# One round of a spectral loop, with two pieces of vector work moved to a later step

## The chip, the cores and the metric

The kernel runs on one core of a Trainium2 chip. The metric is device time in microseconds (us) of one execution. A core has engines with instruction queues of their own, each worked in order: PE (matrix products), DVE and ACT (vector and scalar work), POOL (here copies and the issue of many DMAs) and SP (the issue of other DMAs). They wait for each other through semaphores. The timeline calls a queue's DMA issues SPq, ACTq or POOLq.

## The reference

The reference is a forward pass and its gradients, for one input `x` of 2048 rows by 1024 columns:

```python
g = _sigmoid((x * gate_w).sum(-1, keepdims=True))
a = _A_ref(x, A_w_r, A_w_i)              # irfft2(rfft2(x) * (w_r + 1j * w_i))
b = _B_ref(x, B_w1, B_b1, B_w2, B_b2)    # relu(x @ w1 + b1) ** 2 @ w2 + b2, 3584 hidden
return g * a + (1 - g) * b
```

The outputs are this result and, for a given `grad_out`, the gradients of x, both spectral weights, both MLP weights and biases, and the gate's weights. Here `x` is `A_x`; the MLP's input `B_x` is held constant.

## The kernel before, in words

One main stream of matrix products keeps PE filled: first the MLP's hidden layer and its gradient (`mlp_in`), then the gradients of the weights (`mlp_grads`), then the outputs (`Outputs`). The spectral part is a side stream, a Python generator that is dealt into the main one. `spread` (L1778) runs the main generator and, after each of its yields, advances the side stream by as many steps as are due. While the loop of this change runs beside `mlp_in`, `first_rate` (L1909) makes 1.5 steps due per main yield, so deals of one and of two steps alternate. A main piece is a unit of four yields (`Unit`, L920): seven short chains of four matmuls (tiles ph and pZ, L927) and four chains of eight for the gradient (tile pd, L826). DVE and ACT empty their PSUM banks: DVE writes rT (L946) and dhT (L830), ACT the copies cu and u. A chain that needs a bank waits for that work.

The spectral part has three stages: `first_stage` transforms rows, `fft_mid` (L333) does the column transform, multiplies by the filter and goes back, and `fft_out` transforms the rows back. `fft_mid` is a loop of `NM` = 16 rounds (L532), each for a pair of row groups m and 32 - m, in eight steps with a yield behind each. Each round handles two halves of the columns, h = 1 (which the change's words call the first) and then h = 0. In a round before the change:

- Step 1: `spectra` (L431) multiplies the sums pm and z of both halves into px on PE, after the main stream's last matmul; `grads_of_w` (L493) of the last round's half 0 on DVE (g, gs); `transform` (L441) copies px of half 1 to x on ACT; the loads of next round's z, half 1, are issued on ACT's queue (L404).
- Step 2: the same transform and loads for half 0.
- Step 3: `products` (L448) of half 1, two DVE multiplications of x by the filter w into tt; `by_groups` (L407) reorders the filter of half 0 on POOL (L410, L417).
- Step 4: `rows_of` (L468), the back products of the previous round's y on PE into pv, both halves; `copy_of` (L477) copies half 1 of pv to vc on ACT; results of the weights' gradient are scaled and stored; `filters` (L388) issues loads on POOL's queue.
- Step 5: `joined` (L456), which adds the products to y, half 1; `back` (L483), two DVE operations from pv and vc to pc, and the store of pc to `y_scr` on POOL's queue (L491).
- Step 6: `grads_of_w` of half 1; `mirrored` (L420), sum and difference of next round's z of half 1 on DVE (L426), the difference in place; vc of half 0.
- Step 7: `mirrored` for half 0; `back` of half 0.
- Step 8: `products` and `joined` of half 0; the filter of next round's half 1 on POOL; more scaling.

px and pv share two PSUM buffers (tag `ps2`), so the px of a half also follows the pc that empties the pv of that half. x, w, z, y, pm and pc have two buffers each, tt one, which `grads_of_w` shares (its tile g).

The program text isn't the order of an engine's queue. The build lays out the queues from the data dependences, with the text's order as priority and its own estimate of times, so an operation that it takes to be ready can go ahead of an earlier one. `after`, `behind` and `in_turn` (L250 to L264) add order edges without a wait. The mirrored sums of half 1 have such an edge behind `summed`, the last of `grads_of_w`; px has one behind the main stream's last matmul.

Of the kernel before, what the change touches and what calls it, by code (L numbers as in the profile page):

```python
# [141 lines left out]
def kernel(  # L142
# [98 lines left out]
    def columns_of(scr, c, h):  # L241
        return scr[:].rearrange("t c r x h l -> c h (r x) t l")[c, h]
# [7 lines left out]
    def after(ins, earlier, wait=mybir.DependencyClass.Sync):  # L250

        if earlier is not None:
            info = mybir.DependencyInfo(wait, mybir.DependencyReason.DATA)
            tc.add_manual_dep(ins.ins, earlier.ins.name, info, reason="paced")
# [5 lines left out]
    def behind(ins, eng):  # L260
        after(ins, ahead[eng], mybir.DependencyClass.NoSync)
# [71 lines left out]
    def fft_mid(filler):  # L333
# [63 lines left out]
        def inputs(m, h, copied=None):  # L397
            z = fb.tile([P, 2, 2, HW], FDT, name="z", tag="z", bufs=2)
            for n, c in enumerate((m, R1 // 2 + m)):
                from_ = columns_of(z_scr, c, h)  # L400
                if copied is None:
                    ld(out=z[:, n], in_=from_)
                else:
                    after(nc.scalar.dma_start(out=z[:, n], in_=from_), copied, mybir.DependencyClass.NoSync)  # L404
            return z

        def by_groups(h, wn):  # L407

            w = fb.tile([P, 3, WL], BF16, name="w", tag="w", bufs=2)
            first_ = G.tensor_copy(  # L410
                out=w[:, 0:2, 0:HW].rearrange("p c (g i) -> p c g i", g=4),
                in_=wn[:, :, h * HW : (h + 1) * HW].rearrange("p c (i g) -> p c g i", g=4),
            )
            after(first_, later["mats"], mybir.DependencyClass.NoSync)
            if h:
                after(G.tensor_copy(out=w[:, 0:2, HW], in_=wn[:, :, H]), first_, mybir.DependencyClass.NoSync)
            G.tensor_scalar(out=w[:, 2, 0 : HW + h], in0=w[:, 1, 0 : HW + h], scalar1=-1.0, scalar2=None, op0=ALU.mult)  # L417
            return w

        def mirrored(m, z, summed=None):  # L420

            if m == 0:
                return z[:, 0], z[:, 1]
            pm = fb.tile([P, 2, HW], FDT, name="pm", tag="pm", bufs=2)
            for out, op in ((pm[:], ALU.add), (z[:, 1], ALU.subtract)):
                mixed = V(out=out, in0=z[:, 0], in1=z[:, 1], op=op)  # L426
                behind(mixed, "DVE")
                after(mixed, summed, mybir.DependencyClass.NoSync)
            return pm[:], z[:, 1]

        def spectra(m, pm):  # L431
            px = fps.tile([P, 2, 2, HW], FP32, name="px", tag="ps2", bufs=2)
            for c in range(2):
                for n in range(2):
                    one = mm(px[lanes[n], c], lhsT=mats[m][:, 0, n, lanes[c]], rhs=pm[n], start=True, stop=True)
                    behind(one, "PE")
                    if c + n == 0:
                        in_turn(one, "PE")
            return px

        def transform(m, h, px, ex):  # L441
            x = fb.tile([P, 3, 2, WL], FDT, name="x", tag="x", bufs=2)
            nc.scalar.copy(out=x[:, 1:3, :, 0:HW], in_=px[:])
            copied = nc.scalar.mul(out=x[:, 0, :, 0:HW], in_=px[:, 1], mul=-1.0)
            after(nc.scalar.copy(out=x[:, :, :, h * HW], in_=ex[:, m, :, :, h]), copied, mybir.DependencyClass.NoSync)  # L445
            return x, copied

        def products(h, x, w):  # L448
            tt = fb.tile([P, 2, 2, 2, WL], FDT, name="tt", tag="tt")
            W = HW + h  # L450
            for k, (a, b) in enumerate(((1, slice(0, 1)), (0, slice(1, 3)))):
                by = w[:, b, 0:W].rearrange("p (o t) l -> p o t l", o=1).to_broadcast([P, 2, 2, W])
                V(out=tt[:, k, :, :, 0:W], in0=x[:, a : a + 2, :, 0:W], in1=by, op=ALU.mult)  # L453
            return tt
# [13 lines left out]
        def rows_of(m, y):  # L468
            pv = fps.tile([P, 2, 2, HW], FP32, name="pv", tag="ps2", bufs=2)
            for c in range(2):  # L470
                for n in (1, 0):
                    one = mm(pv[:, n], lhsT=mats[m][lanes[n], 1, c, :], rhs=y[lanes[n], c], start=c == 0, stop=c == 1)
                    if c == 0 and n:
                        in_turn(one, "PE")
            return pv

        def copy_of(m, pv):  # L477
            if m == 0:
                return None, None
            vc = fb.tile([P, 2, HW], FP32, name="vc", tag="vc")  # L480
            return vc, nc.scalar.copy(out=vc[:], in_=pv[:, 1])

        def back(m, h, pv, vc):  # L483
            pc = fb.tile([P, 2, 2, HW], FDT, name="pc", tag="pc", bufs=2)
            if m == 0:
                nc.scalar.copy(out=pc[:], in_=pv[:])
            else:
                V(out=pc[:, 0], in0=pv[:, 0], in1=vc[0][:], op=ALU.add)  # L488
                V(out=pc[:, 1], in0=pv[:, 0], in1=vc[0][:], op=ALU.subtract)
            for n, c in enumerate((m, R1 // 2 + m)):  # L490
                st(out=columns_of(y_scr, c, h), in_=pc[:, n])  # L491

        def grads_of_w(h, x):  # L493
            W = HW + h
            XA, XB = x[:, 0:2, 0, 0:W], x[:, 1:3, 1, 0:W].unsqueeze(1).to_broadcast([P, 2, 2, W])
            part, *inner = XA.ap
            XA = bass.AP(tensor=XA.tensor, offset=XA.offset, ap=[part, inner[0], *inner])
            gs = fb.tile([P, 2, WL], FDT, name="gs", tag="gs", bufs=2)
            t_ = fb.tile([P, 2, 2, 2, WL], FDT, name="g1", tag="tt")[:, 0]
            V(out=t_[:, :, :, 0:W], in0=XB, in1=XA, op=ALU.mult)  # L500
            summed = V(out=gs[:, ::-1, 0:W], in0=t_[:, :, 0, 0:W], in1=t_[:, :, 1, 0:W], op=ALU.add)
            return gs, summed
# [16 lines left out]
        z = {1: inputs(0, 1)}  # L519
# [7 lines left out]
        w = {1: by_groups(1, wn[0])}  # L527
        z[0] = inputs(0, 0)
        pm = {h: mirrored(0, z[h]) for h in (1, 0)}
        x, y, gs, was = {}, {}, {}, None  # L530
        yield
        for m in range(NM):  # L532
            more = m + 1 < NM
            px = {h: spectra(m, pm[h]) for h in (1, 0)}
            if m:
                gs[0], _ = grads_of_w(0, x[0])
            x[1], copied = transform(m, 1, px[1], ex)
            if more:
                z = {1: inputs(m + 1, 1, copied)}
            yield  # L540
            x[0], copied = transform(m, 0, px[0], ex)
            if more:
                z[0] = inputs(m + 1, 0, copied)
            yield
            tt = products(1, x[1], w[1])
            w[0] = by_groups(0, wn[m])
            yield
            if m:
                pv = {h: rows_of(m - 1, y[h]) for h in (1, 0)}
                vc = copy_of(m - 1, pv[1])  # L550
                grads_out(m - 1, 0, gs[0], gw, copied)
            if more:
                wn[m + 1] = filters(m + 1)
            yield
            eh = fb.tile([P, 2, 2], FDT, name="eh", tag="eh")
            y[1] = joined(1, tt, eh)
            if m:
                back(m - 1, 1, pv[1], vc)
            yield
            gs[1], summed = grads_of_w(1, x[1])  # L560
            if more:
                pm = {1: mirrored(m + 1, z[1], summed)}
            if m:
                vc = copy_of(m - 1, pv[0])
            yield
            if more:
                pm[0] = mirrored(m + 1, z[0])
            if m:
                back(m - 1, 0, pv[0], vc)
            yield  # L570
            tt = products(0, x[0], w[0])
            y[0] = joined(0, tt, eh)
            if more:
                w[1] = by_groups(1, wn[m + 1])
            gw = fb.tile([P, 2, LW], BF16, name="gw", tag="gw", bufs=2)
            grads_out(m, 1, gs[1], gw, vc[1] if m else None)
            yield
        gs[0], _ = grads_of_w(0, x[0])
        yield
        for h in (1, 0):  # L580
            pv = rows_of(NM - 1, y[h])
            vc = copy_of(NM - 1, pv)
# [1387 lines left out]
```

## Time and profile before

| What | us |
|---|---|
| median of 3 runs | 1192.29 |
| lowest and highest of them | 1190.86, 1193.34 |
| the profiled execution, its own time | 1196.52 |
| its span, first to last instruction | 1194.7 |
| PE busy in the span | 1173.5 |
| DVE busy in the span | 897.9 |
| first and last start of px in the trace | 225.1, 561.9 |

The trace is one execution. A timeline line gives start, duration, engine, source line, operation, the tile written and those read, the partitions and elements, and, in brackets, how long the engine was idle just before and what ended that. A line of waits gives the engine and line that waited, for whom, the total, how often and the longest. A line of a helper stands for all its callers; L426, for instance, is both the sum (`pm`) and the difference (`z`) in `mirrored`. Some matmul records are missing from the trace, a few per cent, so a chain of eight can show as seven, and PE's idle time is a little overstated.

### The profile page before, as it was taken

What the parts mean: (1) busy time and instruction counts of PE and PEld (TensorE: products, weight loads), DVE (VectorE), ACT (ScalarE), POOL (GpSimd) and SP (SyncE); (2) the same over time, 40 slices, a digit from 0 to 9 for tenths busy, and PEclk for the clock granted to TensorE, in tenths of its full rate; (3) what the DMA queues carried; (4) which work ended last, traced back from release to release, by engine and by line L of the source; (5) the groups of instructions that cost most, each with busy time, mean ns of one, the idle gap of its engine ahead of it and who ended that gap; (6) DMA issues with size and microseconds to landing.
All of it is one profiled execution on the core that took longest, in us unless ns stands there. A gap on an engine that the chain in (4) does not pass through costs nothing.

```text
span 1194.7 us, 19383 instructions
## 1 busy us (share of the span) xinstructions
PE 1173.5 (98%) x7181; PEld 640.3 (54%) x7275; DVE 897.9 (75%) x1598; ACT 531.0 (44%) x961; POOL 387.9 (32%) x618
## 2 busy tenths in 40 slices
PE   8999999999999999999999999999999999999998
PEld 5555555444433444444446999998544444444444
DVE  6898887788988797877537666676786777976757
ACT  5678788577676773445224665664210010000000
POOL 0233443556666683764231333221001100000000
PEclk9999999999999999999999999999999999999999
DMA  9997675687979879889997999995889998564530
GB/s 264 287 306 215 187 203 167 196 219 180 206 186 198 253 250 184 200 187 219 208 198 165 238 226 251 243 216 153 258 188 267 238 277 272 176 194 149 180 124 36
DMA packets 329464, 249.84 MB, mean 209 GB/s; under 512 B 187912, under 2 KB 287658, under 8 KB 328858
## 3 DMA queue, kind: packets, MB, share of 16 engines
q1 hardware_dynamic: 268352, 112.12, 45.1%
q0 software_dynamic: 35136, 111.72, 29.6%
q10 hardware_dynamic: 25882, 24.76, 7.1%
q8 instruction: 57, 0.93, 0.3%
q14 instruction: 37, 0.30, 0.1%
HBM read 114.82 MB, written 89.67 MB: 171 GB/s over the span
## 4 chain that ended last, share of the span: by engine, by line
PE 69%; DVE 16%; DMA 5%; ACT 4%; issue 4%; POOL 1%; SPq 1%; ACTq 0%; another core or an unknown queue 0%; DVEq 0%; POOLq 0%
PE pX L1256 15%; PE xX L1557 14%; PE pV L1256 11%; PE pd L826 8%; PE xV L1557 7%; PE ph L927 4%; PE xZ L1557 3%; PE ph L819 2%; DVE rT L946 2%; DVE dhT L830 1%; DVE tt L453 1%; PE pui L325 1%; PE pki L634 1%; DMA z<-z_scr 1%; PE pu L325 1%
## 5 line engine op out<-in xcount | busy, mean ns | idle before, releaser
L826 PE MATMUL pd<-dbT,w2T 128*128 128x512 bf16 x860 | 206.5, 379 | 7.8 <-DVE rT L946 2.5
L826 PEld LDWEIGHTS <-w2T 128*128 128x128 bf16 x896 | 86.3, 98 | 110.4 <-issue 10.3
L1557 PEld LDWEIGHTS <-dS 128*128 128x128 f16 x686 | 66.4, 98 | 79.4 <-issue 3.8
L830 DVE SCALAR_TENSOR_TENSOR dhT<-pd,rT 128x512 bf16<-128x512 f32 x112 | 76.6, 684 | 31.6 <-PE pd L826 29.2
L1608 POOL DMA_DIRECT2D out_dram<-ot x32 | 17.4, 544 | 248.6 <-DVE ot L1664 128.0
L1674 ACT ACTIVATE w2br<-w2br,dsc 128x512 f32<-128x512 bf16 x8 | 5.8, 723 | 178.6 <-DVE ot L1664 117.4
L1557 PE MATMUL xX<-oT,dS 128*128 128x512 f16 x336 | 76.4, 379 | 0.6 <-DVE eR L1586 0.5
L1272 ACT COPY u<-pX 128x512 f32<-128x512 f32 x56 | 32.8, 586 | 90.8 <-PE pX L1256 85.2
L1557 PEld LDWEIGHTS <-odd 128*128 128x128 bf16 (+1 forms) x462 | 44.8, 98 | 51.5 <-issue 0.9
L1557 PEld LDWEIGHTS <-even 128*128 128x128 bf16 (+1 forms) x448 | 43.6, 98 | 52.6 <-issue 0.7
L1256 PEld LDWEIGHTS <-T 128*128 128x128 f16 x672 | 64.6, 98 | 7.5 <-issue 0.2
L947 ACT ACTIVATE rT<-rT 128x512 bf16<-128x512 bf16 x69 | 43.4, 629 | 50.2 <-DVE rT L946 49.8
L794 ACT ACTIVATE h2T<-rT 128x1024 bf16<-128x1024 bf16 x56 | 59.6, 1064 | 0.2
L1276 DVE TENSOR_TENSOR whi<-pV,u 128x512 bf16<-128x512 f32 x28 | 19.3, 689 | 47.1 <-ACT u L1272 47.0
L1256 PEld LDWEIGHTS <-S 128*128 128x128 f16 x336 | 32.5, 98 | 40.8 <-DVE S L1188 1.9
L491 POOL DMA_DIRECT2D y_scr<-pc x64 | 47.2, 738 | 18.1 <-DVE pc L488 11.1
L453 DVE TENSOR_TENSOR tt<-x,w 128x1028 f16<-128x1028 f16 (+1 forms) x64 | 42.6, 699 | 10.5 <-ACT x L445 4.5
L1256 PEld LDWEIGHTS <-resL 128*128 128x128 bf16 x448 | 43.1, 98 | 4.9
L1256 PEld LDWEIGHTS <-resR 128*128 128x128 f16 (+1 forms) x448 | 42.9, 98 | 4.9 <-issue 0.2
L1276 DVE TENSOR_TENSOR wlo<-pV,u 128x512 bf16<-128x512 f32 x28 | 19.2, 687 | 32.0 <-PE pV L1256 31.9
L858 POOL DMA_DIRECT2D h2T_scr<-h2T x28 | 20.9, 746 | 66.9 <-ACT f L285 29.2
L239 POOL DMA_DIRECT2D r<-y_scr x48 | 28.0, 588 | 41.9 <-ACT re L613 33.1
(382 smaller groups left out, 2798.0 us busy)
## 6 DMA issues: line engine op xcount, KB each, us to landing
h2T_scr<-h2T POOLq DMA_DIRECT2D x28, 512.0 KB, 4.3
dhT_scr<-dhT POOLq DMA_DIRECT2D x28, 512.0 KB, 6.0
y_scr<-pc POOLq DMA_DIRECT2D x64, 128.0 KB, 4.3
ax_scr<-yo POOLq DMA_DIRECT2D x16, 512.0 KB, 5.1
out_dram<-ot POOLq DMA_DIRECT2D x31, 256.0 KB, 3.7
z<-z_scr ACTq DMA_DIRECT2D x60, 128.0 KB, 4.2
out_dram<-whi POOLq DMA_DIRECT2D x28, 256.0 KB, 4.9
out_dram<-wlo POOLq DMA_DIRECT2D x28, 256.0 KB, 5.6
```

The costliest lines, as they stand in the source:

```text
L239: st(out=a, in_=b) if stored else st(out=b, in_=a)
L453: V(out=tt[:, k, :, :, 0:W], in0=x[:, a : a + 2, :, 0:W], in1=by, op=ALU.mult)
L491: st(out=columns_of(y_scr, c, h), in_=pc[:, n])
L794: after(nc.scalar.activation(h2T, rT, ACT.Square), behind_, mybir.DependencyClass.NoSync)
L826: turn["PE"] = mm(pd[:], lhsT=w_[:, ec, fc % FGC * P : (fc % FGC + 1) * P], rhs=dbT[:, ec, ss], start=(ec == 0), stop=(ec == DC - 1),)
L830: return STT(out=dhT, in0=pd[:], scalar=2.0, in1=rT, op0=ALU.mult, op1=ALU.mult, accum_out=gb1part[:, fc, sb : sb + 1],)
L927: turn["PE"] = mm(acc[:], lhsT=lhs[:, t, :], rhs=rhs[:, t, :], start=start and t == 0, stop=t == KH - 1, skip_group_check=True,)
L947: nc.scalar.activation(rT, rT, ACT.Relu)
L1256: self.mm = mm(out, lhsT=lhs[:, t, m * P : (m + 1) * P], rhs=rhs[:, t, :], start=start and t + a == 0, stop=t == KH - 1, skip_group_check= ...
L1272: turn["ACT"] = nc.scalar.copy(out=t_[:], in_=self.X[:])
L1276: turn["DVE"] = self.added = V(out=self.half(row, j), in0=self.sums(acc), in1=self.sums(t_), op=ALU.add)
L1557: ins = mm(acc, lhsT=lhs[:, fc, :], rhs=rhs[:, fc, :], start=start and fc == 0, stop=fc == KH - 1 and bias is None, skip_group_check=True,)
```

## The change

In every round, `products` of half 1 goes from step 3 to step 4, where it stands ahead of the back products; step 3 keeps only the reordering of the filter. The copy vc of half 0 stays in step 6; `back` of half 0 stays in step 7 and becomes its first work. The mirrored sums of half 1 go from step 6 to step 7, behind `back`, and those of half 0 from step 7 to step 8, ahead of the products and the join there. A round keeps eight steps.

```diff
@@ -542,9 +542,9 @@
             if more:
                 z[0] = inputs(m + 1, 0, copied)
             yield
+            w[0] = by_groups(0, wn[m])
+            yield
             tt = products(1, x[1], w[1])
-            w[0] = by_groups(0, wn[m])
-            yield
             if m:
                 pv = {h: rows_of(m - 1, y[h]) for h in (1, 0)}
                 vc = copy_of(m - 1, pv[1])
@@ -558,16 +558,16 @@
                 back(m - 1, 1, pv[1], vc)
             yield
             gs[1], summed = grads_of_w(1, x[1])
+            if m:
+                vc = copy_of(m - 1, pv[0])
+            yield
+            if m:
+                back(m - 1, 0, pv[0], vc)
             if more:
                 pm = {1: mirrored(m + 1, z[1], summed)}
-            if m:
-                vc = copy_of(m - 1, pv[0])
             yield
             if more:
                 pm[0] = mirrored(m + 1, z[0])
-            if m:
-                back(m - 1, 0, pv[0], vc)
-            yield
             tt = products(0, x[0], w[0])
             y[0] = joined(0, tt, eh)
             if more:
```

More of the change, by code (lines that the diff above doesn't have):

```diff
@@ L544, in fft_mid @@
             yield
-            tt = products(1, x[1], w[1])
             w[0] = by_groups(0, wn[m])
             yield
+            tt = products(1, x[1], w[1])
             if m:
@@ L560, in fft_mid @@
             gs[1], summed = grads_of_w(1, x[1])
-            if more:
-                pm = {1: mirrored(m + 1, z[1], summed)}
             if m:
@@ L565, in fft_mid @@
             yield
+            if m:
+                back(m - 1, 0, pv[0], vc)
+            if more:
+                pm = {1: mirrored(m + 1, z[1], summed)}
+            yield
             if more:
                 pm[0] = mirrored(m + 1, z[0])
-            if m:
-                back(m - 1, 0, pv[0], vc)
-            yield
             tt = products(0, x[0], w[0])
```

## The prediction, made before the changed kernel ran

> **What bounds the kernel now.** I read the page first, then the busy time by stretches, then the waits of PE and of DVE in the stretch that the change touches, then the timeline around the longest of them. The page's first part, and the table by stretches (span part, then busy us of PE, PEld, DVE, ACT, POOL, then clock and DMA):
>
> ```profile
> PE 1173.5 (98%) x7181; PEld 640.3 (54%) x7275; DVE 897.9 (75%) x1598; ACT 531.0 (44%) x961; POOL 387.9 (32%) x618
> ...
> 225.00:450.00 225.00, 217.83 (x1049) 93.05 (x1070) 195.48 (x413) 162.48 (x288) 146.56 (x224) 1.00 0.82 208
> 450.00:575.00 125.00, 123.75 (x592) 53.60 (x600) 96.95 (x150) 51.59 (x101) 67.29 (x94) 1.00 0.92 198
> ```
>
> PE is idle for 1194.7 - 1173.5 = 21.2 us of the whole span; that is all that any reordering can win. The loop `for m in range(NM)` (L532) runs from the first px at 225.1 us to past the last at 561.9. Its first twelve rounds lie beside the units of the MLP (225 to 450), where PE is idle 7.2 us and DVE is busy 195.48 of 225, 87%. The later rounds lie beside the weight gradients, where PE is idle 1.25 us in 125. So only 225 to 450 can pay much. PE's waits there (who waited for whom: us in total, times, longest):
>
> ```profile
> PE pd L826 <- DVE rT L946: 2.5, 3, 1.5
> PE pd L826 <- DVE dhT L830: 2.5, 5, 0.7
> PE ph L927 <- ACT u L934: 0.6, 2, 0.3
> PE ph L927 <- DVE rT L946: 0.4, 1, 0.4
> ```
>
> They sum to 6.0 us. None is a wait for the spectral work itself: PE stands because DVE is late with the main stream's rT and dhT, which free PE's banks. Why is DVE late? Its own waits in the same stretch:
>
> ```profile
> DVE pm L426 <- DMA z<-z_scr: 5.0, 4, 2.7
> DVE tt L453 <- issue: 4.5, 3, 2.0
> DVE tt L453 <- ACT x L445: 4.2, 5, 1.3
> DVE tt L453 <- POOL w L410: 0.9, 1, 0.9
> ```
>
> 14.6 us in which the in-order DVE stands at a mirrored sum or at a product of the first half, with rT and dhT queued behind. The longest, first on DVE, then on PE:
>
> ```profile
> 377.42 0.42 DVE L426 TENSOR_TENSOR pm<-z 128x512 f16<-128x512 f16 x1
> 380.55 0.42 DVE L426 TENSOR_TENSOR pm<-z 128x512 f16<-128x512 f16 x1 [2.71 <-DMA z<-z_scr]
> 380.89 0.74 DVE L946 SCALAR_TENSOR_TENSOR rT<-pZ,b1col,cu 128x512 bf16<-128x512 f32 x1
> ```
> ```profile
> 378.28 1.89 PE L927 MATMUL ph<-dbn,Sw 128*128 128x512 f16 x8
> 381.69 1.89 PE L826 MATMUL pd<-dbT,w2T 128*128 128x512 bf16 x8 [1.51 <-DVE rT L946]
> 383.91 1.02 PE L927 MATMUL ph<-dbn,Sw 128*128 128x512 f16 x4 [0.34 <-ACT u L934]
> ```
>
> The sum waits 2.71 us for z (its last transfer was issued at 369.81 and took over 10 us; the stretch's median is 4.7), rT stands behind it, and PE loses 1.51 and then 0.34 us.
>
> **The change part by part.** No instruction, byte or buffer is added or removed. The eight steps of a round keep their number, so the dealing of steps to the main stream is as before. Moved are per round: four mirrored sums (two pairs; one follows the next in 0.34 us) and two products (0.69 each). No DMA changes its step: the loads of z (ACT's queue, steps 1 and 2), the filters and the stores of gw (POOL) stay; the stores of y on POOL come with their pc, which now stands ahead of the sums. SP issues nothing of it.
>
> *Mirrored sums behind pc.* I trace each PE stall back along DVE to the last idle in front of it. Behind waits for z: 0.40 at 259.24 (after 0.39 idle), 0.60 at 318.88 (after 1.45), 1.51 + 0.34 at 381.69 and 383.91 (after 2.71). Sum 2.85 us. After the change the two pc, ready by then (vc was copied before the sums in the last two), run first: 2 x 0.60 = 1.2 us of useful work inside the wait. At 252.92 pc is ACT's (round 0's rows), and a dhT of the main stream fills the 0.39. The 0.43 at 358.90 closes; of the 1.45 there remain 0.25 and of the 2.71 some 1.5, unless the main stream's rT, now of an earlier step, also goes first; then nothing reaches PE. The stalls that remain are bounded by 0 and by 1.85 - 1.2 = 0.65; I take 0.3. Gain 2.55.
>
> *Products beside the back products.* Behind a late tt stand 0.37 at 288.93, 0.71 at 329.47, 0.51 at 350.57, 0.26 and 0.36 at 392.32 and 393.06: 2.21 us. A step later helps only if a piece of the main stream lies between steps 3 and 4. Steps are dealt 1.5 to a main yield, so one round in three has both in one deal; these are the rounds with px at 302.2, 364.1 and 426.1, and their products (307.10, 368.89, 430.21) have no wait. In the others a main piece comes between. The waits are 0.28 to 0.96 us, less than the 2 to 3 us of a deal, so they should close. The joined y1 takes tt a step later still, so nothing reads tt too soon. I take 2.0, not 2.21, as DVE has no less to do.
>
> *What is late next: px.* The two sums of the second half now stand in step 8, directly ahead of products and join, and px of the next round (step 1) reads them. Before, the last thing that px waits for was the pc of step 7. In the three rounds named, steps 8 and 1 come in one deal and there is no slack:
>
> ```profile
> 301.42 0.68 DVE L489 TENSOR_TENSOR pc<-pv,vc 128x512 f16<-128x512 f32 x1
> 302.02 0.74 DVE L946 SCALAR_TENSOR_TENSOR rT<-pZ,b1col,cu 128x512 bf16<-128x512 f32 x1
> 302.68 0.68 DVE L830 SCALAR_TENSOR_TENSOR dhT<-pd,rT 128x512 bf16<-128x512 f32 x1
> ...
> 302.23 0.40 PE L435 MATMUL px<-pm,ab 128*64 128x512 f16 x1
> ```
>
> pc ends at 302.10 and px starts at 302.23. With the second pair taken out (2 x 0.34) pc would end at 301.4, then rT and dhT to 302.7, then the pair to 303.4: px 1.2 us later. If the px matmuls keep their place in PE's queue, that is a stall; if the build puts the next chain of the main stream ahead, it is none. The bounds are 0 and 3 x 1.2 = 3.6. The nearest row is PE's waits above, where no px stands at all; so I take a third, 1.2 us. Of the nine px that wait for a pc of DVE (283.1 to 447.4) five more start 2.3 to 2.6 us behind it and one 6.6, which covers the pair.
>
> *A fuller step 8.* Its DVE work grows from 2.1 to about 2.8 us. At 339.34 PE stands 0.66 us for a dhT behind y, pc, pc, g, gs, pm, pm, z with no idle DVE at all: crowding alone costs that much. It may go (pm leaves that crowd) or come again elsewhere; bounds -0.66 and twice 0.66; I take +0.6.
>
> Sum: -2.55 - 2.0 + 1.2 + 0.6 = -2.75 us. PE is busy 99% from 450 to 1100 us, so what it gains by 450 should reach the end. The profiled execution took 1196.52 us (span 1194.7, 1.8 around it): it would take 1193.8. It lies 4.2 above the median of the runs, 1192.29, so the forecast is **1189.5 us**.
>
> *A rule that speaks against it.* POOL's copies of w lengthen DVE's work beside them: g (L500) takes 0.69 us alone and 1.07 at 275.00, where the copy L410 starts at 275.51 and itself takes 1.08 and not 0.65. Step 8 also issues the copies for the next round, so the second pair now stands nearer to them. [...]
>
> **The rivals.** (1) *px waits for the second pair in every round: slower.* In the five rounds with 2.3 us of slack or a little more, the pair could fall behind rT, dhT and the reduction gb (0.66 + 0.61 + 1.21), and its own 0.68: 3.2 us against 2.3 of slack, a stall of 0.9. The eight cost 3 x 1.2 + 5 x 0.9 = 8.1; with the gain of 4.55 that is +3.55, 1195.8 us. It decides from 0.57 us a round for a loss at all (4.55 / 8), and 0.87 for one over 2.4 us. For it: DVE is busy without a break from 299.8 to 305. Against: PE waits for px nowhere today.
> (2) *The order hardly changes, or the stalls only move.* The built order isn't the text's: at 377.42 and 380.55 the first sums of both pairs stand together, ahead of the second sum of the first pair, so the build fills DVE by its own estimate and may do so again. Gain and loss then cancel: about 1192.0.
> [...]
>
> **How the numbers follow.** A measurement of this kernel tells about 0.2% from no change, 2.4 us: faster is below 1189.9, slower above 1194.7. Chances: the forecast, with its own range 1186.3 (all 5.96 us of stalls gone) to 1189.9, 0.47; rival 1 0.28; rivals 2 and 3 0.19 and 0.06. The forecast lies only 0.4 inside the bound. The range goes from 1186.0 to 1197.0, which takes in every bound of the terms and rival 1. Faster 0.47, same 0.25, slower 0.28.
>
> **What would show it.** Right: in 225 to 450 DVE's waits for z and its tt waits fall from 14.6 us to under 5, PE's waits for rT and dhT from 5.4 to under 3, and the two pc stand ahead of the pm rows. Wrong: a wait of PE, or a long one of ACT's x, at px; pm rows still ahead of pc; a new wait of tt or y; or stalls gone before 450 while PE's idle grows after it.

## The result, and the profile after

The changed kernel took 1197.78 us (median of 18 runs, 1193.84 to 1204.47); the kernel before, run between them on the same chip, 1194.78 (18 runs, 1190.86 to 1200.29). The ratio is 1.0035 [1.0018, 1.0052]: slower. The forecast was 1189.5, with a range from 1186.0 to 1197.0. Two more measurements of the same pair, on two chips, gave 1.0022 [1.0001, 1.0043] and 1.0020 [1.0002, 1.0038] (`after_again`, `after_third` below). The profiled execution took 1195.94 us, its span is 1194.1 and its granted clock (the share of PE's full clock rate that the profile records) 1.000.

The page's first part and the table by stretches of the changed kernel:

```profile
PE 1178.3 (99%) x7275; PEld 640.1 (54%) x7275; DVE 897.4 (75%) x1598; ACT 530.3 (44%) x961; POOL 387.9 (32%) x618
...
225.00:450.00 225.00, 218.75 (x1068) 92.89 (x1065) 195.45 (x412) 161.80 (x288) 147.31 (x222) 1.00 0.78 206
450.00:575.00 125.00, 123.72 (x599) 53.50 (x598) 96.34 (x149) 50.81 (x100) 65.82 (x94) 1.00 0.92 198
```

This execution tells little by itself: the stretch 225 to 450 looks like before's (PE records are more complete, 7275 and not 7181, so PE's busy time can't be compared). The waits tell more. PE's, in that stretch:

```profile
PE pZ L927 <- DMA w1g<-in_B_w_dram: 1.9, 1, 1.9
PE pd L826 <- DVE dhT L830: 1.5, 3, 0.7
PE pd L826 <- DVE rT L946: 1.3, 1, 1.3
PE px L435 <- DVE z L426: 0.6, 1, 0.6
PE ph L927 <- DVE rT L946: 0.4, 1, 0.4
PE ph L927 <- ACT cu L934: 0.3, 1, 0.3
```

The waits for rT and dhT fell from 5.4 to 3.2 us (1.5 + 1.3 + 0.4), as hoped. But three waits are new: px waits once for the second sums (303.70, 0.55 us), a chain of ph once for the copy cu (348.82, 0.27 us), and PE waits 1.9 us for w1g, weights of the MLP, which the change doesn't touch. DVE's waits in the stretch:

```profile
DVE tt L453 <- issue: 5.8, 4, 2.0
DVE tt L453 <- ACT x L445: 4.2, 5, 1.3
DVE Sw L916 <- DMA w1g<-in_B_w_dram: 2.0, 1, 2.0
DVE pm L426 <- DMA z<-z_scr: 1.7, 1, 1.7
```

The waits of the products (tt) are 10.0 us, where they were 9.6: nothing closed. The wait for z is 1.7, and was 5.0.

Why is w1g late? SP's queue, first before, then after (start, duration, queue, line, operation):

```profile
359.05 0.37 SPq L849 DMA_DIRECT2D w1g<-in_B_w_dram  x1
360.76 12.44 SPq L183 DMA_TRANSPOSE w2T<-in_B_w_dram  x2
```
```profile
359.14 9.20 SPq L183 DMA_TRANSPOSE w2T<-in_B_w_dram  x2
368.43 0.53 SPq L849 DMA_DIRECT2D w1g<-in_B_w_dram  x1
```

The load of w1g for the next pair of units stood ahead of the two transposed loads of w2T and now stands behind them. Issuing the two occupies SP for 9.20 us, so w1g starts 9.4 us later. It also lands more slowly, in 8.2 us and not 6.3, and PE stands:

```profile
376.63 1.04 PE L927 MATMUL pZ<-xT,w1g 128*128 128x512 bf16 x4 [1.86 <-DMA w1g<-in_B_w_dram]
```

The built queues, set side by side, show the whole of the change. PE's order is the same to the last matmul. On DVE the pc stand ahead of the next pair's sums, and the second pair behind rT or dhT. On POOL the stores of y stand earlier, and on ACT one copy cu stands behind an rT that it stood ahead of. The products of half 1 have not moved at all. On SP two loads of w1g have changed places with two pairs of transposes, near 297 and near 359 us. The text of neither was touched.

### The profile page after: what moved, and what is told of

The parts are those of the page before. It is cut to its first block, busy times and chain, and to the rows that moved or that the text cites. A ratio compares the mean times of both kernels' runs of the same rounds, so it can differ in the third digit from the quotient of the medians.

```text
span 1194.1 us, 19478 instructions
## 1 busy us (share of the span) xinstructions
PE 1178.3 (99%) x7275; PEld 640.1 (54%) x7275; DVE 897.4 (75%) x1598; ACT 530.3 (44%) x961; POOL 387.9 (32%) x618
## 4 chain that ended last, share of the span: by engine, by line
PE 73%; DVE 16%; issue 4%; ACT 3%; DMA 3%; ACTq 0%; POOL 0%; DVEq 0%; POOLq 0%
PE pX L1256 15%; PE xX L1557 14%; PE pV L1256 11%; PE pd L826 9%; PE xV L1557 7%; PE ph L927 4%; PE xZ L1557 3%; PE ph L819 2%; DVE rT L946 2%; DVE dhT L830 2%; DVE tt L453 1%; PE pui L325 1%; PE pki L634 1%; PE pt L708 1%; PE pu L325 1%
## 5 line engine op out<-in xcount | busy, mean ns | idle before, releaser
L826 PE MATMUL pd<-dbT,w2T 128*128 128x512 bf16 x896 | 210.1, 379 | 3.2 <-DVE dhT L830 1.5
```

What stands on the lines that cost most here:

```text
L826: turn["PE"] = mm(pd[:], lhsT=w_[:, ec, fc % FGC * P : (fc % FGC + 1) * P], rhs=dbT[:, ec, ss], start=(ec == 0), stop=(ec == DC - 1),)
```

## The experiments

Theory A: the loss comes from w1g's new place on SP. Rival B: it comes from the new order on DVE (px behind the second sums, fuller steps). Rival C: the clock is lowered in some executions whatever the kernel, and the two kernels differ by chance. The ratios are to the kernel before, run on the same chip between the others. "Runs at a lower clock" are those whose mean granted clock shows 0.999 or less. The experiments were measured in three sets, each on one chip with runs of the kernel before; of these, 38 of 93 are at a lower clock.

### The changed kernel again (after_again)

> The changed kernel as it is, the base of the next three on one chip. All theories: slower than before by about 4 us (1.0035 measured), between 1.5 and 6. In its trace the two loads of w1g that stand behind the w2T transposes on SP's queue are issued some 8 to 13 us behind the first transpose, and PE waits for one of them (1.86 us at 376.63 in the first trace). Theory clock: time follows the granted clock of each run (0.996 to 0.997: 1200 to 1204 us; 1.000: 1194 to 1197), whatever the order.

1197.99 us, 1.0022 [1.0001, 1.0043]; the profiled execution has a span of 1201.7 and a clock of 0.997. PE's timeline, and then stretches around the stand (busy us of PE, PEld, DVE, ACT, POOL, clock, DMA share, GB/s):

```profile
374.42 1.03 PE L927 MATMUL ph<-xT,dbn 128*128 128x512 bf16 x4
381.93 1.89 PE L927 MATMUL pZ<-xT,w1g 128*128 128x512 bf16 x4 [6.49 <-DMA w1g<-in_B_w_dram]
```
```profile
375.00:380.00 5.00, 0.45 (x3) 0.00 (x0) 0.32 (x2) 0.38 (x1) 0.00 (x0) 0.94 1.18 232
380.00:382.00 2.00, 0.07 (x1) 0.07 (x2) 0.09 (x1) 0.00 (x0) 1.49 (x3) 0.50 0.64 253
382.00:384.00 2.00, 2.00 (x5) 0.66 (x6) 2.00 (x6) 0.30 (x1) 2.00 (x5) 0.50 0.62 131
386.00:388.00 2.00, 1.95 (x9) 0.89 (x9) 1.67 (x3) 2.00 (x4) 1.48 (x3) 0.95 0.96 197
388.00:390.00 2.00, 2.00 (x11) 0.89 (x10) 2.00 (x7) 1.31 (x4) 0.56 (x1) 1.00 0.37 113
```

The same wait, 6.49 us this time, and behind it the matmuls of a chain of four take 1.89 and not 1.04 us: the clock column falls to 0.50. Finer stretches place the half rate from 379.4 to 386.2 us, 6.8 us, of which PE works for 4.3 (from 381.93). So this stand was paid twice, by itself and by this half rate: about 2.1 us more, an estimate from half of the 4.3.

### The changed kernel, w1g ahead of the transposes again (after_w1_first)

```diff
+        held = []
...
+            if held:
+                load_w2(*held.pop(), behind_=later["w1_load"])
...
-                load_w2(fg + 1, later["last"])
+                if fg > 3:
+                    held.append((fg + 1, later["last"]))
+                else:
+                    load_w2(fg + 1, later["last"])
```

(`load_w2` takes `behind_`, an order edge without a wait.) The other queues are as in the changed kernel.

> The changed kernel with one edge more: the two w2T transposes stand behind the next load of w1g on SP's queue, as they did before the change; the orders of PE, DVE, ACT and POOL are those of the changed kernel. Theory SP order (the late w1g load is the loss): the loss of about 4 us goes, the time is that of before or up to 2 us below it, and PE has no wait for w1g. Theory px (PE waits at px for the second pair of sums): it stays about 4 us above before. Theory clock: no difference beyond what the clocks of the runs explain.

1196.22 us, 1.0002 [0.9982, 1.0021]. On SP w1g starts at 357.12, the transposes at 357.60; PE's waits have no w1g any more:

```profile
PE pd L826 <- DVE dhT L830: 3.4, 5, 1.0
PE px L435 <- DVE z L426: 0.6, 1, 0.6
PE pd L826 <- DVE rT L948: 0.5, 1, 0.5
```

What is left, 5.6 us with the groups not shown and no stand longer than 1.0, is of the size of before's 6.0. px still waits its 0.56 us while the loss is gone, so px costs little.

### The kernel before, w1g behind the transposes (before_w1_late)

```diff
-            ld(out=w1[fp][:], in_=w1v[:, :, fp * PW : (fp + 1) * PW])
+            after(ld(out=w1[fp][:], in_=w1v[:, :, fp * PW : (fp + 1) * PW]), later.get("w2_load"), mybir.DependencyClass.NoSync)
```

> The kernel before, with one edge more: two loads of w1g stand behind the w2T transposes on SP's queue, as after the change; all other queues are as before. Theory SP order: slower than before by 3 to 6 us, with a wait of PE and of DVE's weight sums for w1g of 2 us or more in the trace. Theory px: no difference, under 1 us. Theory clock: no difference beyond the clocks.

1198.42 us, 1.0017 [0.9997, 1.0038]: not parted from no change by its interval, and less than the 3 to 6 us expected. The trace has the wait, in the old DVE order:

```profile
375.52 1.04 PE L930 MATMUL pZ<-xT,w1g 128*128 128x512 bf16 x4 [1.76 <-DMA w1g<-in_B_w_dram]
```

9 of the 12 runs are at a lower clock.

### The products alone (products_only)

```diff
-            tt = products(1, x[1], w[1])
             w[0] = by_groups(0, wn[m])
             yield
+            tt = products(1, x[1], w[1])
```

> Only the products of the first half go one step later; the mirrored sums stay. The built queues of all five engines, and their waits, are the same as before the change, so every theory expects the time of before within what two samples of one program differ, under 1.5 us; and the tt waits in the trace as before, 9 to 10 us from 225 to 450. It shows how far the measurement of two equal programs can lie apart.

1195.63 us, 0.999 [0.9972, 1.0007]. The built queues and waits are those of the kernel before, and the time is too: by itself this half of the change does nothing.

### The kernel before, w1g waits for the transposes to land (w1_late_waits)

```diff
-            ld(out=w1[fp][:], in_=w1v[:, :, fp * PW : (fp + 1) * PW])
+            after(ld(out=w1[fp][:], in_=w1v[:, :, fp * PW : (fp + 1) * PW]), later.pop("w2_load", None))
```

> The suspected cost made larger: the kernel before, with the two loads of w1g not only behind the w2T transposes on SP's queue but waiting until the second of them has landed. All queues are in the order of before_w1_late. Theory SP order with the clock as a consequence (a long stand of PE for w1g lowers the granted clock behind it, as in the trace of after_again, where PE stood 6.5 us and the clock was then 0.50 for some 6 us): each run stands for w1g 6 us or more in one place, every run has a granted clock of 0.998 or less, and the time is 8 to 14 us above before. Rival, the clock as an independent cause: the time rises by the stand alone, 5 to 7 us, and the share of runs with a low clock stays as in before, about a quarter. Theory px: no difference.

1199.09 us, 1.0042 [1.0021, 1.0063], with DVE's order as before. SP and PE:

```profile
374.32 0.37 SPq L852 DMA_DIRECT2D w1g<-in_B_w_dram  x1
```
```profile
378.67 1.89 PE L930 MATMUL pZ<-xT,w1g 128*128 128x512 bf16 x4 [4.54 <-DMA w1g<-in_B_w_dram]
```

All 12 runs are at a lower clock, against 7 of 23 of the kernel before in the same set. Lateness of w1g alone, without the change and in a larger dose, makes a loss of the change's size and lowers the clock every time, which speaks against C. The forecast of this run was too high: it said 8 to 14 us and a stand of 6 us or more, and the medians are 4.4 us apart with a stand of 4.54.

### Both pairs of sums in step 7 (pairs_together)

`after_w1_first` with the sums of half 0 one step earlier, so that px finds them ready:

```diff
             if more:
                 pm = {1: mirrored(m + 1, z[1], summed)}
-            yield
-            if more:
                 pm[0] = mirrored(m + 1, z[0])
+            yield
             tt = products(0, x[0], w[0])
```

> As after_w1_first (the w1g loads ahead of the transposes), but both mirrored pairs stand in step 7 behind the pc, none in step 8. Theory px: the 0.55 us wait of PE at px, seen near 303 us in every trace of the changed order, goes, and the time falls by about that, 0.5 us below after_w1_first, which the measurement can't tell; so the trace decides. PE's other waits from 225 to 450 stay within 5 to 6 us, as the crowding of DVE behind them is the same. Theory SP order: within 2 us of before.

1195.83 us, 1.0012 [0.9990, 1.0033]: no gain to be seen from px. The wait at px is gone and dhT is late, 3.6 us on PE (3.4 and 4.0 in the two traces of `after_w1_first`). The clock of this execution fell with no long stand ahead of it:

```profile
386.31 1.89 PE L825 MATMUL pd<-dbT,w2T 128*128 128x512 bf16 x8 [0.59 <-DVE dhT L829]
...
392.26 0.38 PE L825 MATMUL pd<-dbT,w2T 128*128 128x512 bf16 x1 [1.48 <-DVE dhT L829]
```
```profile
394.00:396.00 2.00, 2.00 (x6) 0.72 (x5) 0.75 (x1) 2.00 (x4) 1.94 (x4) 0.50 0.82 200
```

### The kernel before, two more traces (before_look_a, before_look_b)

The kernel as it is; the question was whether its own lower clocks follow stands of PE too.

> The kernel before once more, for its trace. Its runs have a granted clock under 0.999 in about a quarter of all cases. If the clock falls behind a long stand of PE, a run with 0.998 or less shows one of 4 us or more in its trace; if it falls by itself, a stretch with a clock under 1.00 stands without one. With a clock of 1.000 it only adds one more sum of PE's waits from 225 to 450: about 6 us, with the z waits anywhere from 0 to 3 us.

> A second trace of the kernel before, for the same question: where a clock of 0.998 or less comes from, and, at 1.000, PE's waits from 225 to 450 (about 6 us expected).

The first took 1193.23 us at clock 1.000; its z wait is 1.1 us and PE's waits in 225 to 450 are 3.9. The second took 1197.45 at 0.997: DVE stood at the mirrored sum, PE behind it, and the half rate followed:

```profile
320.47 0.42 DVE L426 TENSOR_TENSOR pm<-z 128x512 f16<-128x512 f16 x1 [4.50 <-DMA z<-z_scr]
```
```profile
322.39 3.57 PE L826 MATMUL pd<-dbT,w2T 128*128 128x512 bf16 x8 [4.15 <-DVE rT L946]
```
```profile
322.00:324.00 2.00, 1.61 (x4) 0.56 (x4) 2.00 (x6) 1.63 (x4) 2.00 (x4) 0.50 0.47 99
```

So the wait that the change was to cover is real, and worse in some executions than in the one that the prediction read. It stands behind a pair of transposes: the z of this sum were issued beside the pair near 298 us and landed in 10.4 us (median), and beside the pair near 360 us z lands in 10.3 us in the first trace of before, over a median of 4.7 in the whole stretch.

### The transposes apart (before_split, after_split)

If the burst of two transposes makes z and w1g late, a unit between the two should help both kernels, without touching DVE:

```diff
-                load_w2(fg + 1, later["last"])
+                load_w2(fg + 1, later["last"], (0,) if fg > 3 else (0, FGW // 2))
+            elif 3 < fg < FG - 1 and pr == 1 and u.sp == 0:
+                load_w2(fg + 1, later["last"], (FGW // 2,))
```

> The kernel before, with the two w2T transposes of the fifth and sixth group not in one burst but one unit (some 15 us) apart; the order of every queue is as before. Theory (what makes loads late, of z before the change and of w1g after it, is the burst of transposes, 12 us on SP's queue): the z waits of DVE from 225 to 450 fall from 1 to 6 us to under 1.5, no run stands 4 us, fewer than one run in ten has a clock under 0.999, and the time falls by 1 to 3 us. Rival, the z loads are late for another reason (the loads and stores of POOL's queue at the same time): z waits and clocks as before, time within 1 us of before.

1192.49 us, **0.9975 [0.9958, 0.9991]**: faster than both kernels; 2 of 12 runs are at a lower clock. All built queues are in before's order. z lands in 3.7 us (the four loads from 360 to 376; 7.1 to 10.3 in three traces of before), and DVE's waits for it and PE's waits of any kind (225 to 450) are down to:

```profile
DVE pm L426 <- DMA z<-z_scr: 0.6, 2, 0.3
```
```profile
PE pd L826 <- DVE dhT L830: 1.5, 3, 0.7
PE pd L826 <- DVE rT L946: 0.3, 1, 0.3
PE ph L927 <- ACT u L934: 0.2, 1, 0.2
PE ph L927 <- DVE rT L946: 0.2, 1, 0.2
```

> The changed kernel with the same split; one transpose then stands ahead of each of the two w1g loads, not two. Theory burst: w1g is issued about 4 to 6 us earlier than in the changed kernel, PE has no wait for it or under 1 us, and the time is 2 to 4 us below the changed kernel, within 1.5 us of before_split. Rival: the changed order of DVE itself costs about 1 us, which then remains against before_split.

The same edit on the changed kernel: 1193.57 us, 0.9986 [0.9968, 1.0004]; 1 of 12 at a lower clock. Only one transpose now stands ahead of w1g, and PE doesn't wait for it:

```profile
358.49 1.50 SPq L183 DMA_TRANSPOSE w2T<-in_B_w_dram  x1
360.10 2.06 SPq L849 DMA_DIRECT2D w1g<-in_B_w_dram  x1
...
374.02 1.92 SPq L183 DMA_TRANSPOSE w2T<-in_B_w_dram  x1
```

Against the changed kernel in the same set its mean is 3.1 us less (95% interval 1.4 to 4.9). Against `before_split` it is 1.5 more (0.2 to 2.9): what the change built doesn't pay even here. SP still differs between the two, as a transpose stands ahead of w1g only here, so the 1.5 isn't shown to be DVE's alone.

### Two repeats (after_w1_first_2, after_third)

> A second set of runs of after_w1_first, whose first gave 1.0002 (0.9982 to 1.0021) of before. Theory SP order alone: 0.999 to 1.001. Theory that the new order of DVE costs something too: 1.001 to 1.002. In the trace no wait for w1g, the 0.55 us wait at px, and z waits of about 2 us.

1195.53 us, 1.0010 [0.9992, 1.0029]; z wait 2.7, px 0.6, no w1g.

> The changed kernel on the same chip as the other three, so that what the w1g order and the split each take away can be read against it: 1.002 to 1.004 of before, PE standing for w1g 1.9 us or, in a run with a clock of 0.997, 4 us or more.

1196.61 us, 1.0020 [1.0002, 1.0038]; profiled clock 1.000, and PE's wait for w1g:

```profile
PE pZ L927 <- DMA w1g<-in_B_w_dram: 3.6, 1, 3.6
```

The third trace of the changed kernel with that wait (1.9, 6.5, 3.6); none of eight traces with SP's old order has it (`after_w1_first` twice, `pairs_together`, the kernel before three times, `before_split`, the products alone). This 3.6 us stand was not followed by half rate.

## Why the prediction was wrong

**The step that failed: "SP issues nothing of it", "no DMA changes its step".** True of the text, false of the build, which swapped w1g and the transposes on SP. Late w1g cost PE 1.9, 3.6 and 6.5 us in three traces, and half rate behind the longest. Two sets have both the changed kernel and its version with w1g ahead (24 runs of each, and 70 of before): the means are +2.1 us (0.9 to 3.3) and +0.9 (-0.4 to 2.1) to before, so the place of w1g makes 1.2 of it (-0.3 to 2.7), which this pair alone doesn't part from zero. Taken with `before_w1_late` and `products_only` of the same sets (142 runs; one level for each set, one effect for w1g's place and one for DVE's order) it is 1.45 us (0.4 to 2.5), and DVE's order makes 0.8 (-0.2 to 1.8). The clock agrees: in these two sets 16 of 24 runs of the changed kernel are at a lower clock, 6 of 24 with w1g ahead and 31 of 70 of before; 9 of 12 and 12 of 12 are with before's DVE order and w1g late. With the traces this shows A for the larger part. Why the build swapped them was only argued (the new DVE order shifts its estimate of when the last dhT is done, which the transposes follow); it was not tried.

**"Products beside the back products", -2.0: nothing.** The built order didn't move, and the waits stayed (9.6 to 10.0 us). The prediction held rival 2, "the order hardly changes", right for this half only.

**"Mirrored sums behind pc", -2.55: the order came, the gain didn't.** The pc do stand ahead of the sums. The 5.0 us of z waits, however, came from one execution: the five other traces of before's DVE order with the transposes together have 2.2, 1.1, 5.7, 1.3 and 1.3 us, the five of the new order 1.7, 1.9, 0, 2.1 and 2.7. With w1g left out, PE's waits in 225 to 450 are 4.7 us in the mean of the six and 4.7 in the mean of the five. Nor is the smaller z wait of the changed kernel shown to be the sums' new place. In the five traces with w1g behind the transposes, with either order of DVE, no z wait over 0.2 us stands after 300 us; in seven with w1g ahead and the pair together, six have one, the longest of each 1.9 to 4.5 us, `after_w1_first` (2.1 and 2.7 us near 380) among them. So SP's order trades a late z for a late w1g. The time with w1g ahead is not under before's, 1.0002 and 1.0010.

**px, +1.2: 0.55**, in one of the three rounds named, in each of the six traces of the new order (`after_split` included); rival 1 (px in every round) didn't come. The third rival, with its chance of 0.06, wanted 3.4 us more of DVE, 0.38 in each of nine rounds (g took 1.07 us beside a copy of w on POOL at 275.00 and 0.69 without one); the sixty sums from 225 to 575 us take 24.7 to 25.2 us in four traces of before's order and 23.8 to 25.1 in five of the new, so nothing shows for it. **Step 8, +0.6:** not measured by itself. It may be part of the 0.9 that is left; so may dhT's 3.4 us in `after_w1_first` and the 0.3 us for cu, which stands in each trace of the new order and in none of before's. B stays open as a small share.

**The base.** The forecast stood on the 1192.29 of three runs. In the measurement with the changed kernel the same kernel's median was 1194.78, and 1196.43, 1194.67 and 1195.35 in the three later ones. So the miss of 8.3 us is 2.5 of base, 2.75 of gain that didn't come, and 3.0 of loss. A lower clock in 38 of 93 runs of the kernel before (medians 1197.22 at 0.999 and 1198.99 below it, against 1193.74 at 1.000) was not in the sum, where a stand of PE was counted once, and the three times, 1193.34 at most, show no sign of it.

**C falls as a cause by itself:** three of the four lower clocks seen in traces set in during stands of 4.15, 4.54 and 6.49 us, w1g held until the transposes have landed lowers the clock in 12 of 12 runs, and parting the transposes makes it rare (3 of 24 runs, against 13 of 35 of before in that set). The dip of `pairs_together` follows shorter gaps of 0.59, 1.48 and 0.36 us; what it has in common with the others is not shown.

## What to carry to other kernels

A reordering in the text changes what the build's planner lays out, on queues whose text is untouched too, and may change nothing where it was meant to: compare the built order of every queue, the DMA ones above all, before pricing the steps. When an engine waits for a transfer, ask what makes that transfer late; issuing one of two transposed loads a unit later gave 0.9975 [0.9958, 0.9991], where filling the wait gave nothing. Read a stall from several executions before it becomes a term of a sum: this one was between 1.1 and 5.7 us.

## What the runs showed of the hardware

- In stands of PE of 4.15, 4.54 and 6.49 us (`before_look_b`, `w1_late_waits`, `after_again`) the granted clock fell to 0.50, 2.1, 2.2 and 3.9 us after PE stopped, and stayed there for 6.8 us; in and behind stands of 1.76, 1.86 and 3.6 us (`before_w1_late`, `after`, `after_third`) it did not. In `pairs_together` it fell to 0.50 behind gaps of 0.59, 1.48 and 0.36 us. So the length of one stand doesn't settle it; what sets a dip off, and why one came 2.1 us into a stand while a stand of 3.6 us passed without, is not shown.
- Issuing two transposed loads of w2T together held SP's queue for 7.6 to 15.6 us near 359 us (twelve traces), and the four loads of z issued from 360 to 376 us landed in a median of 6.8 to 10.3 us (six traces of the two kernels) and 11.5 to 12.4 us (three with the sums behind pc and w1g ahead); with a unit between the two transposes, in 3.7 us in the kernel before and 5.4 in the changed one.
